# Rope attention and two MLPs on one core: k's high parts sent ahead of the low parts, and a tile of its own for the fifth unit's exponentials

## The chip, the cores and the metric

The program runs on one core of one Trainium2 chip. The metric is the device time of one execution in microseconds; the runs below are three executions of the kernel before.

## The reference, cut to what matters

```python
q_rot, k_rot = rotate(q), rotate(k)            # (4, 8, 576, 64)
scores = (q_rot @ k_rot.transpose(0, 1, 3, 2)) / sqrt(64)
scores = scores - scores.max(-1, keepdims=True)
attn = np.exp(scores)
attn = attn / (attn.sum(-1, keepdims=True) + 1e-09)
x = (attn @ v).transpose(0, 2, 1, 3).reshape(2304, 512)
h = x @ w_in                                   # 512 -> 2048
x = np.where(h >= 1, h, np.where(h <= -1, 0, (h + 1) ** 2 / 4)) @ w_out
h = np.maximum(x @ w_in2, 0)                   # 512 -> 2048
y = (s * h * h + b) @ w_out2
```

## The kernel before

All products are made from float32 numbers split into a high and a low part of the type fp32r, so that one product is three matmuls. Attention comes first, one pair of heads after the other (16 pairs, numbered 0 to 15). A pair has nine units (`UNITS`, line 333, numbered 0 to 8): 128 rows of q of one head each, and in the middle, as unit 4, the last 64 rows of both heads together. A unit goes through these steps:

- `qk` (line 338): TensorE makes a score tile `sc` of 128 by 576 in PSUM (two tiles go around), VectorE its negated row maximum `nm` (line 354), ScalarE the exponentials `p` with their row sums (line 359).
- `tmain` and `trem` (lines 363 and 383): TensorE transposes `p`. `tmain` takes four blocks of 128 columns of a unit, `trem` the remaining 128 columns of two units of a half pair; after unit 4 it also takes those of unit 4 (line 390) and is the last reader of three tiles at once.
- `av`, `inverse`, `finish` (lines 394 to 442): product with v, one over the row sums (`sume`), which GpSimd spreads out into `eb` (line 417) and TensorE transposes into `rm`; ScalarE copies that to `r` (line 433), and VectorE multiplies.

The two heads' units of the same rows share one tile `p` of 2 x 576 columns: units 0 and 1 have the first, units 2 and 3 the second, unit 4 a third, units 5 and 6 a fourth, units 7 and 8 a fifth. All come from one tag with `PB` = 3 buffers.

K of a pair is prepared during the pairs before: GpSimd multiplies and adds (`rope_pair`, line 285), and for every pair but the first `lay_k` (line 310) has ScalarE make the high part, GpSimd the low part, and SyncE's queue send them to where the score matmuls read them: the high part of each head twice to `kh` (line 323, four transfers), the low part of each head once to `kz` (line 324, two transfers). Both have two buffers, so that pair i+2's transfers wait for pair i's last score matmuls.

From unit 48 on (in pair 5) TensorE's stream also gets steps of the first MLP, called fill below (`beside`, line 472: products `h` and `y`, lines 483 and 500), and weights are converted from unit 33 on (`convert`, line 545). After attention the MLPs run alone.

The order of instructions on every engine is set when the program is built: instructions are issued in the order of the main loop (line 635), and a scheduler with its own model of time moves them, within what the tiles' buffers, the priorities and the `issue_after` marks allow. A change of a buffer thus moves instructions on all engines. Each engine then runs its stream strictly in that order.

Of the kernel before, what the change touches and what calls it, by code (L numbers as in the profile page):

```python
# [8 lines left out]
F32 = mybir.dt.float32  # L9
# [10 lines left out]
B, H, S, D = 4, 8, 576, 64  # L20
# [3 lines left out]
P = 128  # L24
# [18 lines left out]
PB = 3  # L43
# [23 lines left out]
def kernel(ctx, tc, qq, kk, vv, tab, ww1, ww2, s, b, out):  # L67
    nc = tc.nc
# [16 lines left out]
    def pool_tt(out, in0, in1, op, dim=-1):  # L85

        n = out.shape[dim]
        free = 1
        for x in out.shape[1:]:
            free *= x  # L90
        k = min(n, -(-free // PW))
        for i in range(k):
            c = [slice(None)] * len(out.shape)
            c[dim] = slice(n * i // k, n * (i + 1) // k)
            c = tuple(c)
            nc.gpsimd.tensor_tensor(out=out[c], in0=in0[c], in1=in1[c], op=op)  # L96
# [142 lines left out]
    att = pa.enter_context(tc.tile_pool(name="att", bufs=1, side="right", reuse_waits="tile"))  # L239
    att2 = pa.enter_context(tc.tile_pool(name="att2", bufs=2, side="right", reuse_waits="tile"))  # L240
# [8 lines left out]
    def bank(name):  # L249
        return ps_b.tile([P, 512], F32, tag="bank", name=name)  # L250
# [34 lines left out]
    def rope_pair(i, nm, mul, add, lo_eng, pieces=WHOLE):  # L285

        t = qk_in.pop((nm, i))
        tt = {nc.gpsimd: pool_tt, nc.vector: nc.vector.tensor_tensor}
        last = None
        for c in pieces:  # L290
            tt[mul](out=t[:, :, c], in0=t[:, :, c], in1=tab_sb[:, :, c], op=ALU.mult)
            r = t[:, 1, c]
            tt[add](out=r, in0=t[:, 0, c], in1=r, op=ALU.add)
            last = (lay_q if nm == "q" else lay_k)(i, t, c, lo_eng)
        return last

    SELF = [slice(0, D), slice(D, P)]
# [12 lines left out]
    def lay_k(i, t, c, lo_engs, heads=range(2)):  # L310
        if c.start == 0 and 0 in heads:
            stacks["k", i] = att.tile([P, 2, S], F32R, tag="kh", name="kh", bufs=2), kz_t[i % 2]
        kh, kz = stacks["k", i]
        tt = {nc.gpsimd: pool_tt, nc.vector: nc.vector.tensor_tensor}
        r = t[:, 1, c]
        if i > 0:
            hi, lo = t[:, 0, c].bitcast(F32R), r.bitcast(F32R)
            nc.scalar.copy(hi, r)
            pool_tt(out=lo, in0=r, in1=t[:, 0, c], op=ALU.subtract)
            for j in range(2):  # L320
                own = SELF[j]
                for rows in SELF:
                    nc.sync.dma_start(out=kh[rows, j, c].bitcast(F32), in_=t[own, 0, c])
                m = nc.sync.dma_start(out=kz[own, j, c].bitcast(F32), in_=t[own, 1, c])
            return m.ins
        for j in heads:
            own, other = SELF[j], SELF[1 - j]
            nc.scalar.copy(kh[own, j, c], r[own])
            m = nc.scalar.copy(kh[other, j, c], r[own])
            tt[lo_engs[j]](out=kz[own, j, c], in0=r[own], in1=kh[own, j, c], op=ALU.subtract)  # L330
        return m.ins
# [3 lines left out]
    p_t, sums_t, u_t = {}, {}, {}  # L335
    pt = {}

    def qk(i, k):
        if k == 0:
            sums_t[i] = att2.tile([P, 9], F32, tag="sums", name="sums")  # L340
        j, t = UNITS[k]
        sc = ps_s.tile([P, 2, 512], F32, tag="sc", name="sc")
        if j is None:
            places = [(0, 512), (1, S + D)]
        else:
            places = [(j, t * P + j * (QW + D))]
        straight = [[(0, 0, 288)], [(0, 288, 288)]]
        moved = [[(0, D, 288)], [(0, 352, 224), (224, 0, D)]]
        for half in range(2):
            todo = [(stacks["q", i][:, c:c + P], r[:, h], w) for h, c in places for r in stacks["k", i] for w in (moved if j is None and h == 0 else straight)[half]]  # L350
            for m, (l, r, (o, k0, n)) in enumerate(todo):
                nc.tensor.matmul(sc[:, half, o:o + n], l, r[:, k0:k0 + n], start=m == 0, stop=m == len(todo) - 1)  # L352
        nm = att.tile([P, 1], F32, tag="nm", name="nm", bufs=4)
        maxs[i * 9 + k] = nc.vector.tensor_reduce(out=nm, in_=sc[:, :, :288], axis=AX.XY, op=ALU.max, negate=True).ins  # L354
        if j != 1:
            p_t[i, t] = att.tile([P, 2 * S], F32, tag="p", name="p", bufs=PB)
        p = p_t[i, t][:, S * (j == 0):S * (j == 0) + S]
        col = 4 if j is None else 2 * t + j + t // 2
        exps[i * 9 + k] = nc.scalar.activation(p, sc[:, :, :288], AF.Exp, bias=nm, scale=1.0, accum_out=sums_t[i][:, col:col + 1]).ins  # L359
        if j is None:  # L360
            nc.scalar.copy(p_t[i, t][:, S:S + D], p[:, 512:])
# [32 lines left out]
    def av(i, g, ps, kts):  # L394

        v, n = v_in[i], GROUPS[g][1]
        r = pt["r", g]
        for kt in kts:
            for j in range(2):
                nc.tensor.matmul(ps[j * D:(j + 1) * D, :n], v[:, kt, j, :], pt[g][:, kt, j, :], start=kt == 0, stop=False)  # L400
        if 3 not in kts:
            return
        if g == 0:
            for j in range(2):
                nc.tensor.matmul(ps[j * D:(j + 1) * D, 256:320], v[:, 4, j, :], r[:, 256 + j * D:320 + j * D], start=False, stop=False)
        for j in range(2):
            nc.tensor.matmul(ps[j * D:(j + 1) * D, :256], v[:, 4, j, :], r[:, :256], start=False, stop=True)

    def inverse(i, g):

        e = att2.tile([P, 5], F32, tag="sume", name="sume")
        sm = sums_t[i]
        m = 5 - g
        nc.scalar.activation(e[:, :m], sm[:, 5 * g:5 * g + m], AF.Identity, bias=eps, scale=1.0)
        nc.vector.reciprocal(e[:, :m], e[:, :m])
        eb = att2.tile([P, 4, D], F32, tag="eb", name="eb")
        nc.gpsimd.tensor_copy(eb, e[:, 0:4].unsqueeze(2).to_broadcast([P, 4, D]))
        return e, eb

    def finish(i, g, e, eb, slices):  # L420
        ps = bank("av")
        for kts in slices:
            av(i, g, ps, kts)
            if 3 not in kts:
                yield
        rm = bank("rm")
        for t in range(2):
            nc.tensor.transpose(rm[:, t * P:(t + 1) * P], eb[:, 2 * t:2 * t + 2, :].rearrange("p j d -> p (j d)"), ident)
        if g == 0:
            nc.tensor.transpose(rm[:, 256:384], e[:, 4:5].to_broadcast([P, P]), ident)  # L430
            u_t[i] = att2.tile([P, S], F32, tag="u", name="u")
        r = att2.tile([P, 384], F32, tag="r", name="r")
        nc.scalar.copy(r[:, :384 - 128 * g], rm[:, :384 - 128 * g])
        u = u_t[i]
        c = slice(256 * g, 256 * g + 256)
        nc.vector.tensor_tensor(out=u[:, c], in0=ps[:, :256], in1=r[:, :256], op=ALU.mult)
        if g == 0:
            nc.vector.tensor_tensor(out=u[:D, 512:], in0=ps[:D, 256:320], in1=r[:D, 256:320], op=ALU.mult)
            nc.vector.tensor_tensor(out=u[D:, 512:], in0=ps[D:, 256:320], in1=r[D:, 320:384], op=ALU.mult)
            return  # L440
        bb, hp = divmod(i, NP)
        nc.sync.dma_start(out=xd[hp, :, bb * S:(bb + 1) * S], in_=u_t.pop(i))
# [79 lines left out]
    QP = [slice(0, P), slice(P, 288), slice(288, S)]  # L522
    turned_by(tk, HALVES[0])
    lay_k(0, tk, HALVES[0], [nc.gpsimd, nc.gpsimd])
    turned_by(tk, HALVES[1])
    lay_k(0, tk, HALVES[1], [nc.gpsimd, nc.gpsimd], [0])
    turned_by(tq, QP[0])
    hi, rest = lay_q(0, tq, QP[0], None, [0])
# [35 lines left out]
    def do_qk(n):  # L564
        if n < len(units):
            i, k = units[n]
            if k == 4:
                pad_v(i)
            qk(i, k)
# [28 lines left out]
    def do_t(n):  # L598
        if LT <= n < len(units) + LT:
            i, k = units[n - LT]  # L600
            tmain(i, k)
            if k in (4, 8):
                trem(i, k // 8)
                rbs[i, k // 8] = inverse(i, k // 8)
# [409 lines left out]
    def cut(n0, n1, n):  # L1014

        k = -(-(n1 - n0) // n)
        at = [n0 + (n1 - n0) // 16 * i // k * 16 for i in range(k + 1)]
        return [(a, b - a) for a, b in zip(at, at[1:])]
# [5 lines left out]
    a, b, c, d = cut(last, NT, N2A), cut(0, last, N2), cut(last, NT, N2), cut(0, NT, N2)  # L1024
# [153 lines left out]
```

## Time and profile before

| what | us |
|---|---|
| median of three runs (1125.59 to 1128.71) | 1128.46 |
| the profiled execution | 1129.47 |
| its span, first to last instruction | 1127.7 |
| TensorE busy | 1078.5 |
| VectorE busy | 786.1 |
| ScalarE busy | 631.1 |
| GpSimd busy | 430.0 |

The exponentials run from 15.5 to 434.1 us; what comes after is the MLPs. In the views, PE is TensorE, PEld its weight loads, DVE VectorE, ACT ScalarE, POOL GpSimd, SP SyncE. L359 is line 359 of the kernel. A line of the timeline has the start, the duration, the engine, and output and inputs by the program's names; a bracket gives the engine's idle time just before and what ended it. The granted clock is 1.00 at 2.4 GHz and 0.50 at 1.2 GHz.

### The profile page before, as it was taken

The page shows a single profiled execution, that of the slowest core. Times are in us where ns is not written, and L with a number is a line of the kernel's source. Part 1 is how long each engine was busy: PE and PEld are TensorE (multiplying, and loading weights), DVE is VectorE, ACT ScalarE, POOL GpSimd, SP SyncE. Part 2 cuts the span into 40 slices and gives each one's busy share as a digit, 9 for nine tenths or more (in the row PEclk, how much of TensorE's full clock was granted, in tenths as well). Part 3 has the DMA queues.
Part 4 walks back from the last instruction along what each step waited for, and adds up shares of the span by engine and source line. Part 5 has one row for each costly group of instructions (what it writes and reads, how often), then busy time and mean ns, then how long its engine had stood idle before and what let it go on. Part 6 is the DMA issues. An engine that isn't in the chain of part 4 may idle for free.

```text
span 1127.7 us, 20049 instructions
## 1 busy us (share of the span) xinstructions
PE 1078.5 (96%) x7296; PEld 986.5 (87%) x7296; DVE 786.1 (70%) x1449; ACT 631.1 (56%) x1430; POOL 430.0 (38%) x564
## 2 busy tenths in 40 slices
PE   3998988889999999999999999999999999999998
PEld 3666677778988989999999999999999999999997
DVE  6888888886676663355656667866877678767754
ACT  4777776765767665555545545465444448334421
POOL 7968886875453240252544454300211120000000
PEclk9999999999999999999999999999999999999999
DMA  7665856646667543745466573322232754221210
GB/s 221 170 183 157 243 162 190 209 150 179 199 196 217 176 157 92 265 128 180 148 222 221 193 233 113 118 74 88 80 127 90 273 183 126 82 69 54 81 62 35
DMA packets 109762, 173.24 MB, mean 154 GB/s; under 512 B 29408, under 2 KB 80608, under 8 KB 109664
## 3 DMA queue, kind: packets, MB, share of 16 engines
q1 hardware_dynamic: 109664, 171.97, 48.8%
q8 instruction: 57, 0.93, 0.3%
q14 instruction: 41, 0.34, 0.1%
HBM read 110.10 MB, written 48.56 MB: 141 GB/s over the span
## 4 chain that ended last, share of the span: by engine, by line
PE 79%; DVE 7%; DMA 4%; ACT 4%; POOL 3%; issue 2%; SPq 1%; POOLq 0%; ACTq 0%; DVEq 0%
PE hps L180 15%; PE sum L914 13%; PE yps L829 6%; PE yps L830 6%; PE yps L828 6%; PE sc L352 5%; PE y L180 4%; PE yps L764 4%; PE yps L766 4%; PE yps L765 4%; PE h L180 4%; PE av L400 3%; PE tp L374 3%; DVE nm L354 1%; POOL kin L96 1%
## 5 line engine op out<-in xcount | busy, mean ns | idle before, releaser
L180 PE MATMUL hps<-xh,w 128*128 128x288 f32 (+4 forms) x640 | 163.4, 324 | 0.0
L354 DVE TENSOR_REDUCE nm<-sc 128x1 f32<-128x576 f32 x144 | 107.9, 752 | 44.9 <-PE sc L352 44.3
L352 PE MATMUL sc<-kh,qs 128*128 128x288 f32 x336 | 104.8, 333 | 32.1 <-ACT p L359 19.7
L359 ACT ACTIVATE p<-sc,nm 128x576 f32<-128x576 f32 x144 | 106.8, 745 | 33.5 <-DVE nm L354 32.7
L922 ACT ACTIVATE four<-four,b_sb,s_sb 128x480 f32<-128x480 f32 x64 | 47.4, 782 | 127.4 <-DVE four L921 127.4
L830 PE MATMUL yps<-gh,w 128*128 128x480 f32 (+1 forms) x320 | 118.5, 370 | 0.0
L829 PE MATMUL yps<-gl,w 128*128 128x480 f32 (+1 forms) x320 | 118.5, 370 | 0.0
L828 PE MATMUL yps<-gh,w 128*128 128x480 f32 (+1 forms) x320 | 118.4, 370 | 0.0
L180 PEld LDWEIGHTS hps<-xh,w 128*128 128x128 f32 x640 | 113.2, 188 | 1.0
L96 POOL TENSOR_TENSOR wm<-wm,w 128x256 f32<-128x256 f32 x80 | 71.5, 913 | 111.9 <-ACT w L138 73.0
L352 PEld LDWEIGHTS sc<-kh,qs 128*128 128x128 f32 x336 | 65.1, 196 | 52.0 <-ACT p L359 28.6
L180 PE MATMUL hps<-xl,w 128*128 128x288 f32 (+4 forms) x320 | 103.7, 324 | 0.0
L352 PE MATMUL sc<-kz,qs 128*128 128x288 f32 x336 | 95.4, 303 | 0.0
L374 PE MATMUL tp<-ident,p 128*128 128x128 f32 x576 | 90.0, 281 | 4.9 <-ACT p L359 3.3
L764 PE MATMUL yps<-gh,w 128*128 128x288 f32 (+3 forms) x288 | 93.2, 324 | 0.7 <-ACT ys L502 0.5
L765 PE MATMUL yps<-gl,w 128*128 128x288 f32 (+3 forms) x288 | 92.8, 322 | 0.0
L766 PE MATMUL yps<-gh,w 128*128 128x288 f32 (+3 forms) x288 | 92.8, 322 | 0.0
L96 POOL TENSOR_TENSOR wm<-wm,raw 128x256 f32<-128x256 f32 x16 | 12.8, 818 | 176.9 <-ACT raw L138 176.9
L374 PEld LDWEIGHTS tp<-ident,p 128*128 128x128 f32 x576 | 72.3, 145 | 8.1 <-ACT p L359 3.7
L180 PE MATMUL y<-gh,w 128*128 128x288 f32 x320 | 75.0, 305 | 3.2 <-DVE ptr L392 2.0
L180 PE MATMUL h<-xh,w 128*128 128x288 f32 x320 | 73.3, 306 | 3.2 <-DVE gl L106 1.8
L400 PE MATMUL av<-pt,vin 128*64 128x256 f32 (+1 forms) x512 | 75.1, 417 | 0.7 <-DVE gl L106 0.7
(154 smaller groups left out, 2891.5 us busy)
## 6 DMA issues: line engine op xcount, KB each, us to landing
wraw<-in_ww SPq DMA_DIRECT2D x56, 512.0 KB, 4.4
w<-parkd SPq DMA_DIRECT2D x24, 512.0 KB, 6.3
kin<-in_k SPq DMA_DIRECT2D x15, 576.0 KB, 5.1
qin<-in_q SPq DMA_DIRECT2D x15, 576.0 KB, 4.5
kh<-kin SPq DMA_DIRECT2D x60, 144.0 KB, 2.6
parkd<-wraw SPq DMA_DIRECT2D x16, 512.0 KB, 3.1
xs<-y1d SPq DMA_DIRECT2D x32, 240.0 KB, 2.7
xd<-u SPq DMA_DIRECT2D x16, 288.0 KB, 2.6
```

The costliest lines, as they stand in the source:

```text
L180: m = nc.tensor.matmul(out_ps, l, r, start=(i == 0), stop=(i == n - 1))
L352: nc.tensor.matmul(sc[:, half, o:o + n], l, r[:, k0:k0 + n], start=m == 0, stop=m == len(todo) - 1)
L354: maxs[i * 9 + k] = nc.vector.tensor_reduce(out=nm, in_=sc[:, :, :288], axis=AX.XY, op=ALU.max, negate=True).ins
L374: m = nc.tensor.transpose(v[:, c, :], p[:, c * P:(c + 1) * P], ident)
L400: nc.tensor.matmul(ps[j * D:(j + 1) * D, :n], v[:, kt, j, :], pt[g][:, kt, j, :], start=kt == 0, stop=False)
L764: nc.tensor.matmul(acc, wh, gh, start=f == 0, stop=False)
L765: nc.tensor.matmul(acc, wh, gl, start=False, stop=False)
L766: nc.tensor.matmul(acc, wl, gh, start=False, stop=last)
L828: nc.tensor.matmul(acc, wh, gh, start=f == 0, stop=False)
L829: nc.tensor.matmul(acc, wh, gl, start=False, stop=False)
L830: nc.tensor.matmul(acc, wl, gh, start=False, stop=last)
L914: nc.tensor.matmul(acc, l, r, start=j == 0, stop=j == len(t) - 1)
```

## The change

Three things change. In `lay_k` all four transfers of the high part are issued first, and the two of the low part are marked to be issued after the last of them. Unit 4's exponentials (576 columns, and a copy of 64 of them) get a tile of their own of 640 columns with one buffer (tag `ends`), and the three buffers of `p` are left to the other units. `eb` and `r` go from two buffers to one; the 2,560 bytes per partition that this frees are those that the new tile takes.

```diff
@@ lay_k
             for j in range(2):
-                own = SELF[j]
                 for rows in SELF:
-                    nc.sync.dma_start(out=kh[rows, j, c].bitcast(F32), in_=t[own, 0, c])
-                m = nc.sync.dma_start(out=kz[own, j, c].bitcast(F32), in_=t[own, 1, c])
+                    m = nc.sync.dma_start(out=kh[rows, j, c].bitcast(F32), in_=t[SELF[j], 0, c])
+            with tc.issue_after(m.ins):
+                for j in range(2):
+                    m = nc.sync.dma_start(out=kz[SELF[j], j, c].bitcast(F32), in_=t[SELF[j], 1, c])
             return m.ins
@@ qk
         if j != 1:
-            p_t[i, t] = att.tile([P, 2 * S], F32, tag="p", name="p", bufs=PB)
+            p_t[i, t] = att.tile([P, 2 * S], F32, tag="p", name="p", bufs=PB) if t < 4 else att.tile([P, S + D], F32, tag="ends", name="p", bufs=1)
@@ inverse
-        eb = att2.tile([P, 4, D], F32, tag="eb", name="eb")
+        eb = att2.tile([P, 4, D], F32, tag="eb", name="eb", bufs=1)
@@ finish
-        r = att2.tile([P, 384], F32, tag="r", name="r")
+        r = att2.tile([P, 384], F32, tag="r", name="r", bufs=1)
```

The counts of instructions on every engine stay as they were. What follows shows how they move. Lines after 320 have other numbers in the changed kernel (359 is 360 there), the numbers behind a name tell tiles of one name apart, and "waits" names the engines (or DMA queues) whose semaphores an instruction waits for; DVE_49 is VectorE, PE_49 TensorE.

ScalarE in pair 1, around the exponentials of units 5 and 6 (tile `p_503`), before:

```order
L361 COPY p_483<-p_483 128x64 [waits Activation_49]
L414 ACTIVATE sume_543<-sums_350,eps_67 128x5
L433 COPY r_518<-rm_515 128x256 [waits PE_49]
L377 COPY pt_441<-tp_532 128x8x64 [waits PE_49]
L359 ACTIVATE p_503,sums_350<-sc_496,nm_501 128x576 [waits PE_49]
L359 ACTIVATE p_503,sums_350<-sc_522,nm_527 128x576 [waits DVE_49]
```

and in the change:

```order
L362 COPY p_483<-p_483 128x64 [waits Activation_49]
L415 ACTIVATE sume_543<-sums_350,eps_67 128x5
L360 ACTIVATE p_503,sums_350<-sc_496,nm_501 128x576 [waits DVE_49]
L434 COPY r_518<-rm_515 128x256 [waits PE_49]
L378 COPY pt_441<-tp_532 128x8x64 [waits PE_49]
L360 ACTIVATE p_503,sums_350<-sc_522,nm_527 128x576 [waits DVE_49]
```

Unit 5's exponential moved ahead of two copies that wait for TensorE, and itself waits for its maximum alone. Before, 17 of the 144 exponentials wait for TensorE, unit 5's of every pair among them; in the change it is 15, none of them in pairs 0 to 6, and in pairs 7 to 15 those of unit 2 or unit 7.

TensorE in pair 7, from unit 6's score tile (`sc_2317`) to unit 7's (`sc_2343`), before:

```order
L352 MATMUL sc_2317<-kz1_110,qs1_108 128x288
L374 MATMUL tp_2327<-ident_101,p_2247 128x128 [waits Activation_49]
L374 MATMUL tp_2327<-ident_101,p_2247 128x128 x3
L387 MATMUL tr_2333<-ident_101,p_2095 128x128 [waits DVE_49]
L387 MATMUL tr_2333<-ident_101,p_2158 128x128
L390 MATMUL tr_2333<-ident_101,p_2247 128x128 [waits Activation_49]
L352 MATMUL sc_2343<-kh_1798,qs1_108 128x288 [waits Activation_49]
```

and in the change, from the transposes of unit 4 (`p_2247`) by way of unit 8's score tile (`sc_2401`) to the first matmul of fill behind:

```order
L375 MATMUL tp_2327<-ident_101,p_2247 128x128 [waits Activation_49]
L375 MATMUL tp_2327<-ident_101,p_2247 128x128 x3
L353 MATMUL sc_2401<-kh_1798,qs1_108 128x288 [waits PE_49,Activation_49]
L353 MATMUL sc_2401<-kz1_110,qs1_108 128x288
L353 MATMUL sc_2401<-kh_1798,qs1_108 128x288
L353 MATMUL sc_2401<-kz1_110,qs1_108 128x288
L388 MATMUL tr_2333<-ident_101,p_2095 128x128 [waits DVE_49]
L388 MATMUL tr_2333<-ident_101,p_2158 128x128
L391 MATMUL tr_2333<-ident_101,p_2247 128x128
L375 MATMUL tp_2374<-ident_101,p_2288 128x128 [waits Activation_49]
L375 MATMUL tp_2374<-ident_101,p_2288 128x128 x3
L180 MATMUL h_2380<-xh_1978,w_1132 128x288 [waits DVE_49]
```

The three last transposes of the first half (`tr_2333`) stood right ahead of unit 7's score tile; now they stand behind unit 8's, and four transposes and twelve matmuls of fill follow before the next pair's first score tile. In pairs 0 to 6 TensorE's transposes stay ahead of unit 7's score tile.

SyncE's queue where pair 4's k is sent (`kin_769`), before:

```order
L324 DMA kz0_109<-kin_769 64x576 [waits DMAHW2_49,PE_49,Pool_49]
L466 DMA xs_1559<-xd_57 128x288 [waits DMAHW7_49,DMAHW3_49]
L323 DMA kh_909<-kin_769 64x576 [waits DMAHW4_49,PE_49]
L323 DMA kh_909<-kin_769 64x576 [waits DMAHW5_49]
L323 DMA kh_909<-kin_769 64x576 [waits DMAHW6_49]
L323 DMA kh_909<-kin_769 64x576
L324 DMA kz0_109<-kin_769 64x576 [waits DMAHW0_49,PE_49]
L261 DMA qin_1263<-in_q 128x1152 [waits DMAHW1_49,DVE_49]
```

and in the change:

```order
L322 DMA kh_909<-kin_769 64x576 [waits DMAHW2_49,PE_49,Activation_49]
L322 DMA kh_909<-kin_769 64x576 [waits DMAHW3_49]
L322 DMA kh_909<-kin_769 64x576 [waits DMAHW4_49]
L322 DMA kh_909<-kin_769 64x576 [waits DMAHW5_49]
L325 DMA kz0_109<-kin_769 64x576 [waits DMAHW6_49,Pool_49]
L325 DMA kz0_109<-kin_769 64x576 [waits DMAHW7_49,PE_49]
L261 DMA qin_1263<-in_q 128x1152 [waits DMAHW0_49,DVE_49]
L467 DMA xs_1559<-xd_57 128x288 [waits DMAHW1_49]
```

The first transfer of the low part went from the head of the group to behind the four of the high part, and so one transfer more lies ahead of the load of q for a later pair (`qin_1263`).

## Rows read from the trace of the kernel before

**Rows 1.** The page's first part: TensorE's busy time, share of the span and instructions.
```profile
PE 1078.5 (96%) x7296; PEld 986.5 (87%) x7296; DVE 786.1 (70%) x1449; ACT 631.1 (56%) x1430; POOL 430.0 (38%) x564
```

**Rows 2.** Stretches: busy time of each engine, instructions in brackets, granted clock, DMA.
```profile
core 0: us, PE busy (x) PEld busy (x) DVE busy (x) ACT busy (x) POOL busy (x), PEclk, DMA share, GB/s
28.00:350.00 322.00, 295.35 (x2177) 242.93 (x2176) 255.78 (x426) 224.59 (x538) 236.91 (x315) 0.98 0.64 188
350.00:1127.70 777.70, 772.82 (x5084) 734.72 (x5082) 511.95 (x997) 393.86 (x865) 172.63 (x217) 1.00 0.42 137
```

**Rows 3.** Waits of TensorE from 28 to 350 us: total, times, longest.
```profile
PE sc L352 <- ACT p L359: 17.2, 17, 2.8
PE y L180 <- POOL w L96: 0.2, 1, 0.2
```

**Rows 4.** ScalarE in order of time, pair 4: start, us, instruction.
```profile
111.26 0.75 ACT L359 ACTIVATE p<-sc,nm 128x576 f32<-128x576 f32 x1
111.99 0.74 ACT L359 ACTIVATE p<-sc,nm 128x576 f32<-128x576 f32 x1
```

**Rows 5.** TensorE at the same place; in brackets the idle time before.
```profile
110.80 0.27 PE L390 MATMUL tr<-ident,p 128*128 128x128 f32 x1
112.15 0.40 PE L352 MATMUL sc<-kh,qs 128*128 128x288 f32 x1 [1.08 <-ACT p L359]
```

**Rows 6.** VectorE at the same place.
```profile
112.99 0.76 DVE L354 TENSOR_REDUCE nm<-sc 128x1 f32<-128x576 f32 x1 [0.66 <-PE sc L352]
```

**Rows 7.** TensorE at the same place of pairs 0 and 5.
```profile
32.16 0.40 PE L352 MATMUL sc<-kh,qs 128*128 128x288 f32 x1 [1.08 <-ACT p L359]
132.63 0.40 PE L352 MATMUL sc<-kh,qs 128*128 128x288 f32 x1 [1.08 <-ACT p L359]
```

**Rows 8.** TensorE at the same place of pairs 7, 8 and 9.
```profile
188.76 0.61 PE L352 MATMUL sc<-kh,qs 128*128 128x288 f32 x1 [2.85 <-ACT p L359]
219.09 0.60 PE L352 MATMUL sc<-kh,qs 128*128 128x288 f32 x1 [2.30 <-ACT p L359]
250.23 0.61 PE L352 MATMUL sc<-kh,qs 128*128 128x288 f32 x1 [1.10 <-ACT p L359]
```

**Rows 9.** Stretches around those waits; the sixth figure is the granted clock.
```profile
185.00:188.40 3.40, 0.91 (x9) 0.67 (x6) 3.40 (x7) 3.23 (x8) 3.00 (x5) 1.00 0.16 44
188.40:191.80 3.40, 3.04 (x13) 3.03 (x14) 3.07 (x7) 2.83 (x8) 3.24 (x4) 0.50 0.16 36
219.20:222.60 3.40, 3.40 (x15) 3.37 (x16) 2.60 (x5) 2.74 (x6) 2.13 (x3) 0.51 0.95 299
249.90:253.30 3.40, 3.07 (x13) 3.06 (x14) 3.33 (x5) 3.23 (x10) 2.90 (x4) 0.51 0.47 121
277.30:280.70 3.40, 3.40 (x17) 3.38 (x16) 1.70 (x5) 2.16 (x7) 3.26 (x6) 0.52 0.26 97
```

**Rows 10.** Chain of waits: twelve matmuls of a fill step in one go.
```profile
297.12 1.59 PE h L180 x12
```

**Rows 11.** SyncE's queue in pair 2, sending pair 4's k.
```profile
72.55 0.53 SPq L324 DMA_DIRECT2D kz<-kin  x1
74.44 2.73 SPq L323 DMA_DIRECT2D kh<-kin  x4
77.28 0.55 SPq L324 DMA_DIRECT2D kz<-kin  x1
```

**Rows 12.** DMA issues, 60 to 190 us: count, KB, median us to landing.
```profile
kz<-kin SPq DMA_DIRECT2D x10, 144.0 KB, 2.7
```

**Rows 13.** TensorE, first matmul of pair 4's first score tile.
```profile
94.92 0.40 PE L352 MATMUL sc<-kh,qs 128*128 128x288 f32 x1
```

**Rows 14.** GpSimd's copy for pair 1's second group, TensorE's last transpose of the first.
```profile
57.42 0.40 POOL L417 COPY eb<-sume 128x256 f32<-128x256 f32 x1 [2.04 <-DVE sume L415]
...
60.03 0.27 PE L430 MATMUL rm<-ident,sume 128*128 128x128 f32 x1
```

**Rows 15.** Waits of GpSimd from 28 to 350 us.
```profile
POOL qin L96 <- DMA qin<-in_q: 24.5, 12, 8.5
```

## The prediction

> **What bounds the kernel now.** I read the page first: TensorE is busy for 1078.5 us of the 1127.7 us span [rows 1], so time can come only from what TensorE stands or runs slowly. The table of stretches says where. From 350 us to the end it stands for 777.7 - 772.8 = 4.9 us; from 28 to 350 us, the attention part, for 322.0 - 295.4 = 26.6 us, at a mean granted clock of 0.98 instead of 1.00 [rows 2]. The other engines have slack there: VectorE is busy for 255.8 of the 322 us, ScalarE for 224.6, GpSimd for 236.9. The list of TensorE's waits in this stretch gives the cause of most of it: 17.2 us in 17 waits end with an exponential on ScalarE, while for GpSimd it stands 0.2 us [rows 3].
>
> The timeline shows what the exponential had waited for. In pair 4, trem's last transpose starts at 110.80 [rows 5]; unit 5's exponential starts at 111.26, unit 6's right behind it at 111.99 [rows 4], though the first needs only a maximum made before. It writes a tile of `p` whose last reader was that transpose. Unit 7's score tile needs the score buffer that unit 5's exponential reads last, and TensorE stands 1.08 us before it at 112.15 [rows 5]. The same wait, 1.08 us, stands in pairs 0 to 5, six times (the first and the last in [rows 7]), and longer in pairs 7, 8 and 9: 2.85, 2.30 and 1.10 us [rows 8]. In other pairs fill lies between and hides it.
>
> **The change part by part.** *The tile of its own.* Unit 5's exponential no longer needs unit 4's tile nor the transposes behind it. In pairs 0 to 6 the order leaves no exponential waiting for TensorE. The wait of pairs 0 to 5 goes: at most 6 x 1.08 = 6.5 us. What is late next is VectorE's maximum, which had stood 0.66 us in pair 4 for that very score tile [rows 6]; the rest of the 1.08 us VectorE spent on work that must be done anyway. I take 6 x 0.66 = 3.9 us, since the steps behind hang on VectorE, and keep 0 (the next step simply waits elsewhere) and 6.5 as ends.
>
> In pairs 7 to 15 the same step is moved, not removed: 15 exponentials (units 2 and 7) there wait for a group of transposes that the order now puts later. What counts is how much TensorE has to do between those transposes and the score tile that needs the exponential. Before, it had nothing in pairs 7 and 8 and nine matmuls (1.59 / 12 x 9 = 1.2 us [rows 10]) in pair 9, so that transposes to score tile took 2.85, 2.30 and 1.10 + 1.2 = 2.3 us [rows 8], 2.5 in the mean. In the changed order 12 of the 15 have a step of twelve matmuls or its worth behind them, 1.59 us, mostly two; three (pair 11, unit 7; pair 13, unit 7; pair 15, unit 2) have about 1.2 us. If all took 2.5 us, the three would cost 3 x 1.3 = 3.9 us and the two with little over 1.6 us (pair 7, unit 7; pair 8, unit 2) about 0.6 each: 5.0 us. As several pairs before hid the wait with as little, I take half, 2.5 us. So of 2.85 + 2.30 + 1.10 = 6.25 us, 3.75 are won; ends 1.25 and 6.25.
>
> *The clock.* Each of the three long waits has a stretch at 1.2 GHz on it: the granted clock is 1.00 from 185.0 to 188.4 us, in which TensorE worked for 0.91 us, and 0.50 from 188.4 to 191.8; so it is again at 219.2 and 249.9, and a fourth time at 277.3, where no exponential was waited for [rows 9]. In the first three TensorE is busy 3.04, 3.40 and 3.07 us; at 2.4 GHz that work takes half, so they cost 1.52 + 1.70 + 1.54 = 4.8 us. I take two of the three, 3.2 us, as the moved order can bring one of its own; ends 0 and 4.8, with the fourth (1.7) 6.5. The Trainium skill ("TensorE: Matmul & The Clock Gate", Part 1: The HAM clock gate) says that the low clock is the default state, which activity lifts and idleness brings back. By that rule all three would go with their waits, 4.8 us instead of 3.2, and the total would be 1117.0; the trace agrees as far as the place goes, since every low stretch begins beside an idle TensorE.
>
> *High parts first.* Nobody waits for these transfers. Pair 4's are issued from 72.55 to 77.28 + 0.55 [rows 11] and land 2.7 us later [rows 12], at 80.5; its first score matmul starts at 94.92 [rows 13]. The first transfer of `kh` must wait for pair 2's last score matmuls anyway, and `kz` ahead of it ran in that pause. Now both `kz` come behind: one transfer, 0.55 us, is added ahead of the next load of q. GpSimd stands 24.5 us in 12 waits for such loads [rows 15], so 12 x 0.55 = 6.6 us more at worst for GpSimd; TensorE waits for GpSimd for 0.2 us in all [rows 3]. I cost it at nothing; what hides it is the lead of more than 14 us that k has, and GpSimd's 322 - 237 = 85 us of idle time.
>
> *One buffer for `eb` and `r`.* `eb` of a pair's second group must now wait for the transposes of the first group's. In pair 1 the copy starts at 57.42 and those transposes end at 60.03 + 0.27 = 60.30 [rows 14]: it would stand 2.9 us. Behind it in GpSimd's queue is the low part of a k that is sent only at 72.55 [rows 11]: 11 us of cover. Nothing, by the same idle time; if that were gone, 16 x 2.9 = 46 us of GpSimd against its 85. `r` is written once in half a pair and read by VectorE within that half: nothing.
>
> **The sum.** 3.9 + 3.75 + 3.2 = 10.9 us. Against the profiled execution, 1129.5 - 10.9 = **1118.6 us**; that execution lies 1.0 us above the median of the runs, which is within what the runs differ by.
>
> **The rivals.**
> - *All of it.* TensorE keeps the whole of the waits, and no low clock replaces the three: 6.5 + 6.25 + 4.8 = 17.5 us, 1112.0; with the fourth stretch and a part of the unrelated waits (26.6 - 17.2 = 9.4 us in the stretch, which a new order shuffles) down to 1109. For it: all other engines have slack in the sums. Against: the steps behind unit 7 are VectorE's.
> - *The stall only moves.* In pairs 0 to 5 VectorE's maximum is met by other work of VectorE, and in pairs 7 to 9 the new waits cost the upper 5.0 us with one or two low stretches: 6.25 - 5.0 + about 0, some 1 us, **1128**. For it: one exponential in ten still waits for TensorE, 15 against 17 before. Against: the 15 are those with fill behind them.
> - *Slower, by the late transposes.* Trem now stands behind two score tiles in most of pairs 7 to 15, and the fill that should hide the wait has inputs from ScalarE's same queue, in which the exponential stands. If it stands too, the cover is gone. With seven of the 15 uncovered at the mean of rows 8, 2.08 us, that is 14.6 us, and 7 x 1.6 = 11.2 us of low clock; less 3.9 + 6.25 + 4.8 = 14.95 that go, 10.9 us slower, **1140.4**. It decides from about four uncovered waits on: 4 x (2.08 + 1.6) = 14.7. Against: before, no wait with twelve matmuls behind it showed.
> - *The first part does something.* It can't help: the data lie there 14 us early.
>
> **How the numbers follow.** A measurement here can tell about 0.3%, 3.4 us, from no change. My forecast has 0.46, with a range of its own from 1114 to 1124; all of it 0.18; the moved stall 0.20; slower 0.16. Faster by over 0.3% (under 1125.1): 0.46 + 0.18 + 0.02 of the moved stall = 0.66; the rest of it, 0.18, is within; slower 0.16. The range leaves out the slower case and a little below: 1109 to 1130.
>
> **What would show it.** Right, if the trace after has: unit 5's exponential apart from unit 6's in pairs 0 to 6, with no wait of TensorE of 1.08 us before unit 7's score tile; the sum of TensorE's waits on exponentials from 28 to 350 us at half of 17.2 us or less; one or two low-clock stretches instead of four; and the span from 350 us on unchanged. Wrong, if waits of 1 us and more stand before the first or the third score tile of pairs 8 to 15, if VectorE's idle time in the first 150 us does not fall, or if GpSimd's wait for `rm` at `eb` reaches TensorE.

## The result, and the profile after

The changed kernel takes 1114.26 us in the median of four runs (1113.05 to 1114.57), the kernel before 1127.03 us beside it (1125.18 to 1128.71): a ratio of **0.9883, 95% interval 0.9865 to 0.9901**. The forecast was 1118.6 us. The profiled executions differ by 1129.47 - 1114.57 = 14.9 us, the medians by 12.8, and the readings below are made against the 14.9 of the profiles.

The page's first part and two lines of its table of groups, changed kernel (to [rows 1]; in a group's line the last figures are idle time before it and what ended most of it):

```profile
PE 1074.0 (97%) x7296; PEld 982.0 (88%) x7296; DVE 778.2 (70%) x1449; ACT 628.5 (56%) x1430; POOL 431.1 (39%) x564
...
L360 ACT ACTIVATE p<-sc,nm 128x576 f32<-128x576 f32 x144 | 106.7, 743 | 32.1 <-DVE nm L355 29.5
...
L355 DVE TENSOR_REDUCE nm<-sc 128x1 f32<-128x576 f32 x144 | 106.7, 749 | 22.6 <-PE sc L353 21.9
```

VectorE's maxima stand 21.9 us for score tiles; the same line of the kernel before had this:

```profile
L354 DVE TENSOR_REDUCE nm<-sc 128x1 f32<-128x576 f32 x144 | 107.9, 752 | 44.9 <-PE sc L352 44.3
```

The stretches, changed kernel, as in [rows 2], and then split where pair 6's first exponential starts:

```profile
28.00:350.00 322.00, 306.55 (x2300) 252.16 (x2300) 260.69 (x449) 233.03 (x563) 243.83 (x322) 1.00 0.66 198
350.00:1112.80 762.80, 757.22 (x4964) 721.14 (x4960) 499.80 (x976) 382.81 (x840) 167.44 (x210) 1.00 0.41 136
28.00:134.34 106.34, 102.60 (x740) 74.43 (x739) 96.38 (x157) 82.22 (x193) 96.71 (x125) 1.00 0.69 198
134.34:1112.80 978.46, 961.16 (x6522) 898.87 (x6520) 664.10 (x1267) 533.61 (x1212) 314.55 (x408) 1.00 0.46 149
```

The same split of the kernel before:

```profile
28.00:141.74 113.74, 103.97 (x753) 74.52 (x751) 98.32 (x160) 83.24 (x194) 96.01 (x127) 1.00 0.67 189
141.74:1127.70 985.96, 964.19 (x6508) 903.14 (x6506) 669.42 (x1264) 535.21 (x1210) 313.53 (x406) 0.99 0.46 148
```

This split is the sum in measured form. A stretch's length less TensorE's busy time is its idle time. Up to pair 6 TensorE's idle time falls from 9.8 to 3.7 us and its busy time by 1.4, as 13 of its instructions now come later. Behind that point idle time falls from 21.8 to 17.3 us and busy time by 3.0, although the 13 instructions are added. Together: 6.0 + 4.5 = 10.5 us of idle time and 4.4 us of busy time. The instructions are the same 7296, so the 4.4 us are instructions that ran faster: the granted clock is 1.00 in every stretch, and none of the four stretches of [rows 9] is left. (The record of the clock begins at 28.0 us in the kernel before and at 31.0 in the changed one. Up to there a score matmul with `kz` takes 0.44 us, behind it 0.29 to 0.30, so the changed kernel's first 3 us in the table are slow ones that the figure 1.00 does not show.)

The waits of TensorE from 28 to 350 us, changed kernel, its two longest sums (to [rows 3]), and of GpSimd's those of [rows 14, 15]:

```profile
PE sc L353 <- ACT p L360: 7.0, 10, 1.4
PE tp L375 <- DVE pt L382: 2.6, 3, 1.7
...
POOL qin L96 <- DMA qin<-in_q: 19.5, 8, 8.1
...
POOL eb L418 <- PE rm L429: 4.4, 3, 2.4
```

TensorE waits for exponentials 7.0 us instead of 17.2. The three longest of these waits that are left:

```profile
110.51 0.40 PE L353 MATMUL sc<-kh,qs 128*128 128x288 f32 x1 [1.20 <-ACT p L360]
...
124.39 0.40 PE L353 MATMUL sc<-kh,qs 128*128 128x288 f32 x1 [0.82 <-ACT p L360]
...
180.15 0.40 PE L353 MATMUL sc<-kh,qs 128*128 128x288 f32 x1 [1.42 <-ACT p L360]
```

The first stands at the end of pair 4, for unit 7's exponential, where the kernel before has no such wait; the last stands in pair 7, for unit 6's. The place itself, in pair 2 of the changed kernel (exponentials of units 5 and 6; TensorE's last transpose of `trem` and unit 7's score tile; VectorE's maxima of units 6 and 7), to be held against [rows 4 to 6]:

```profile
67.27 0.74 ACT L360 ACTIVATE p<-sc,nm 128x576 f32<-128x576 f32 x1 [0.72 <-DVE nm L355]
68.73 0.77 ACT L360 ACTIVATE p<-sc,nm 128x576 f32<-128x576 f32 x1
...
68.22 0.27 PE L391 MATMUL tr<-ident,p 128*128 128x128 f32 x1
68.25 0.38 PE L353 MATMUL sc<-kh,qs 128*128 128x288 f32 x1
...
67.85 0.71 DVE L355 TENSOR_REDUCE nm<-sc 128x1 f32<-128x576 f32 x1
69.28 0.74 DVE L355 TENSOR_REDUCE nm<-sc 128x1 f32<-128x576 f32 x1
```

Unit 5's exponential starts 0.95 us ahead of the last transpose and 1.46 us ahead of unit 6's (0.73 before), so that unit 7's score tile follows the transpose without a pause, where 1.08 us stood.

### The profile page after: what moved, and what is told of

It reads as the page before. It is cut to its first block, busy times and chain, and to the rows that moved or that the text cites. A ratio compares the mean times of both kernels' runs of the same rounds, so it can differ in the third digit from the quotient of the medians.

```text
span 1112.8 us, 20049 instructions
## 1 busy us (share of the span) xinstructions
PE 1074.0 (97%) x7296; PEld 982.0 (88%) x7296; DVE 778.2 (70%) x1449; ACT 628.5 (56%) x1430; POOL 431.1 (39%) x564
## 4 chain that ended last, share of the span: by engine, by line
PE 82%; DVE 7%; DMA 3%; ACT 3%; POOL 3%; issue 2%; SPq 0%; POOLq 0%; ACTq 0%; DVEq 0%
PE hps L180 15%; PE sum L915 14%; PE yps L831 6%; PE yps L830 6%; PE yps L829 6%; PE y L180 5%; PE sc L353 5%; PE yps L765 4%; PE av L401 4%; PE yps L767 4%; PE yps L766 4%; PE h L180 4%; PE tp L375 3%; DVE nm L355 2%; ACT p L360 1%
## 5 line engine op out<-in xcount | busy, mean ns | idle before, releaser
L355 DVE TENSOR_REDUCE nm<-sc 128x1 f32<-128x576 f32 x144 | 106.7, 749 | 22.6 <-PE sc L353 21.9
L96 POOL TENSOR_TENSOR wm<-wm,raw 128x256 f32<-128x256 f32 x16 | 12.8, 819 | 176.5 <-ACT raw L138 176.5
L375 PEld LDWEIGHTS tp<-ident,p 128*128 128x128 f32 x576 | 70.8, 143 | 10.2 <-ACT p L360 3.7
L106 DVE TENSOR_TENSOR gl<-hps,gh 128x288 fp32r<-128x288 f32 (+4 forms) x88 | 46.5, 528 | 40.5 <-ACT gh L102 40.4
```

What stands on the lines that cost most here:

```text
L375: m = nc.tensor.transpose(v[:, c, :], p[:, c * P:(c + 1) * P], ident)
```

## The experiments

The theory: the tile of its own makes the gain, in two places, by the waits of pairs 0 to 5 and by those of pairs 7 to 9 with their stretches at 1.2 GHz; the other two parts are worth nothing. The rivals: one of the other parts does something; or the tile does nothing in one of the places, and the gain there is that of another order of instructions, since the scheduler moves instructions on all engines after any edit. So the first five kernels (e1 to e5) are parts of the change; the rest test the order (by a second rate of fill), the size of the early gain, and more cover. The kernels with the tile in some pairs only (e3, e4, e9, e12) have the other two parts as well.

All results in one table. "Begins" is the start of pair 6's first exponential, "behind" the rest of the span; "idle" (TensorE's idle time) and "1.2 GHz" are for that rest, the latter by the record of the granted clock, without the end of the program. "Unit 5" is the sum of TensorE's waits (0.15 us and longer) from pair 7 on that end with an exponential of unit 5, as read from each trace. All these are of one profiled execution; the ratio is that of the runs to the kernel before.

| kernel | tile in pairs | begins | behind | idle | unit 5 | 1.2 GHz | ratio (95%) |
|---|---|---|---|---|---|---|---|
| before | none | 141.7 | 986.0 | 21.8 | 6.8 | 13.7 | 1 |
| e2_kz_only | none | 139.8 | 988.5 | 24.1 | 7.2 | 13.7 | 1.0033 (1.0019 to 1.0046) |
| e5_single_only | none | 141.5 | 989.6 | 23.1 | 7.1 | 20.5 | 1.0043 (1.0027 to 1.0059) |
| e6_before_fill | none | 141.2 | 986.0 | 25.6 | 3.5 | 3.4 | 1.0033 (1.0021 to 1.0045) |
| e4_late_only | 7 to 15 | 143.0 | 982.1 | 18.6 | 0.5 | 13.7 | 1.0002 (0.9989 to 1.0015) |
| e9_three | 0 to 2 | 135.7 | 991.2 | 23.6 | 6.2 | 20.5 | 1.0006 (0.9991 to 1.0022) |
| e3_early_only | 0 to 6 | 134.9 | 983.3 | 19.7 | 5.1 | 10.2 | 0.9925 (0.9902 to 0.9948) |
| e12_early_fill | 0 to 6 | 133.6 | 985.5 | 23.7 | 3.5 | 3.4 | 0.9966 (0.9948 to 0.9984) |
| the changed kernel | all | 134.3 | 978.5 | 17.3 | 0.6 | 0 | 0.9883 (0.9865 to 0.9901) |
| e1_no_kz | all | 134.8 | 986.1 | 20.7 | 0 | 13.7 | 0.9946 (0.9925 to 0.9967) |
| e7_after_fill | all | 134.3 | 982.0 | 19.7 | 0 | 6.8 | 0.9909 (0.9893 to 0.9925) |
| e8_nokz_fill | all | 133.2 | 983.2 | 19.2 | 0 | 10.2 | 0.9912 (0.9897 to 0.9926) |
| e10_fill80 | all | 135.5 | 984.2 | 21.7 | 0 | 10.2 | 0.9954 (0.9940 to 0.9968) |
| e11_fill70 | all | 133.7 | 993.8 | 26.1 | 0 | 20.5 | 1.0036 (1.0020 to 1.0052) |

### The parts, one by one

**k's transfers in the old order, all else as changed (e1), and the new order alone (e2).** In e1 the two `kz` transfers go back between those of `kh`, as the minus lines of the change's first hunk have them; e2 is the kernel before with the plus lines of that hunk alone.

> The changed kernel with the transfers of k put back into their old order; the tile of its own and the single buffers stay. Theory (the gain is the exponential's wait and the clock on it; nobody waits for k's transfers): as fast as the changed kernel, 1113 to 1116 us, no 1.08 us wait in pairs 0 to 5, none or one low-clock stretch. Rival (sending the high parts first is part of the gain): 1118 us or more.

> The kernel before with k's high parts sent first and nothing else changed. Theory: no change, 1125.5 to 1129 us, with the waits of 1.08 us in pairs 0 to 5 and three or four low-clock stretches still there. Rival (the transfers give part of the gain): 1123 us or less.

Measured: 1120.96 us and 1131.45 us. Neither fits the theory, and e1's time is what the rival had said: without the part the changed kernel loses 6.7 us. But alone the part loses 0.33%. Two signs for one edit do not speak for an effect on the chip; they speak for the order. That is put to the test by e7 and e8 below.

**The tile in the early pairs alone (e3), in the late ones alone (e4).** In pairs without it unit 4 takes one of the three tiles `p`, as before. This is e3's condition; e4 has `i < 7` in the place of `i > 6`.

```diff
...
-if t < 4 else att.tile([P, S + D], F32, tag="ends", name="p", bufs=1)
+if t < 4 or i > 6 else att.tile([P, S + D], F32, tag="ends", name="p", bufs=1)
```

> The changed kernel with unit 4's own tile in pairs 0 to 6 only; from pair 7 on unit 4 takes one of the three buffers of p again. Theory: the early part of the gain alone, 4 to 8 us, so 1119 to 1123 us; pair 6 begins at about 134 us as in the changed kernel; unit 5's exponential waits again in pairs 7 to 9 and the low-clock stretches there are back. Rival (the gain is not in the waits but in the new order of conversions and fill behind): the gain is not split, 1115 us or less, or 1126 and more.

> The changed kernel with unit 4's own tile from pair 7 on only. Theory: the late part of the gain alone, 5 to 9 us, so 1118 to 1122 us; six waits of 1.08 us in pairs 0 to 5 as in the kernel before, and none or one low-clock stretch behind. Rival: as for the run before, 1115 us or less, or 1126 and more.

Measured: 1119.87 us and 1126.78 us. The split of e3's profile, and of e4's:

```profile
28.00:134.90 106.90, 101.08 (x734) 72.37 (x733) 97.11 (x157) 81.54 (x191) 95.81 (x125) 1.00 0.68 197
134.90:1118.20 983.30, 963.64 (x6522) 903.30 (x6521) 664.97 (x1267) 534.54 (x1212) 316.02 (x408) 0.99 0.47 148
```

```profile
28.00:142.96 114.96, 103.85 (x744) 74.78 (x743) 101.06 (x162) 84.36 (x195) 97.21 (x129) 0.99 0.65 187
142.96:1125.10 982.14, 963.55 (x6518) 903.50 (x6516) 661.26 (x1263) 533.55 (x1210) 311.33 (x404) 0.99 0.46 148
```

E3 is as expected: pair 6 begins as early as in the changed kernel, and what lies behind is nearer to the kernel before. Unit 5's exponential is waited for again in pairs 7 and 8 (2.35 and 2.09 us), though not in pair 9. E4 missed its time. Its split shows 982.1 us behind pair 6 against 986.0, and unit 5's late waits are down to 0.5 us; but it runs 13.7 us at 1.2 GHz there, as the kernel before does, where at most one stretch had been expected. It gives 1.2 us back in pairs 0 to 5, where it should be as before, and the medians show no gain (1.0002). The change in the early part is worth most; the late one needs a better test (e12).

**One buffer for `eb` and `r` alone (e5).** The kernel before with `bufs=1` at both, as in the change.

> The kernel before with eb and r at one buffer each and nothing else changed. Theory (GpSimd's wait for the transposes is hidden by its idle time): no change, 1125.5 to 1130 us, GpSimd waits for rm at eb for some 3 to 10 us in all, and TensorE for GpSimd for under 1 us. Rival (that wait reaches TensorE): 1132 us or more.

Measured: 1132.94 us. Waits of GpSimd from 28 to 350 us in e5, the one of this kind that the kernel before has there, and those of TensorE in e5:

```profile
POOL eb L417 <- PE rm L430: 11.9, 1, 11.9
...
POOL eb L417 <- PE rm L428: 6.8, 1, 6.8
```

```profile
POOL eb L417 <- PE rm L430: 5.5, 1, 5.5
```

```profile
PE sc L352 <- ACT p L359: 18.9, 15, 3.5
...
PE y L180 <- POOL w L96: 0.2, 1, 0.2
```

The waits for `rm` are there, 18.7 us in two where the kernel before stands 5.5 once, and one is 11.9 us long where the prediction had 2.9. The time is one that the rival had said (1132 or more). But TensorE still waits for GpSimd for 0.2 us in all, so the wait does not reach it directly; what grew is TensorE's waits for exponentials, 18.9 us instead of 17.2, and its time at 1.2 GHz, 23.9 us in all instead of 13.7. The miss is of the size of an order drawn anew, and this part alone was not run at a second order: that the single buffers cost some of the 0.43% is not excluded.

### Is it the order? A second rate of fill

`run_fill` sets how many steps of fill are let in for each unit, 0.62 in pairs 5 to 8 and 0.92 behind. A slightly other rate leaves the work as it is and makes the scheduler draw the order behind the start of pair 6 anew: in the traces TensorE's order first differs at 150.7 us between the kernel before and e6, and at 144.7 us between the changed kernel and e7, and that of the other engines later still. So these kernels test the late part; the early part has the same order at both rates. Three kernels with the new rate stand to each other as before, after and e1 do.

```diff
-            run_fill(0.62 if n < 76 else 0.92)
+            run_fill(0.6 if n < 76 else 0.9)
```

> The kernel before with the fill per unit at 0.6 and 0.9 instead of 0.62 and 0.92, which hardly changes the work beside attention but makes the scheduler find another order from pair 5 on. It is the base of the two runs that follow. Theory (what follows pair 6 depends on the order that is found, by some 4 us either way): 1123 to 1132 us, pair 6 begins at 140 to 143 us. Rival (the order does not matter by itself): 1126 to 1129 us.

> The changed kernel with the same fill. Theory: pair 6 begins at 134 to 136 us as in the changed kernel, 6 to 8 us earlier than in the run before; the rest is 976 to 988 us by the order found, so 1111 to 1124 us in all. Rival (the tile and the high parts first together bring what the changed kernel showed, whatever the order): 1113 to 1116 us, and no low-clock stretch.

> The same fill, with the tile and the single buffers, and k's transfers in the old order. Theory (the transfers' order matters only through the order of everything else that the scheduler finds): pair 6 begins at 134 to 136 us; the total lies within 4 us of the run before, on either side. Rival (high parts first is worth some 6 us beside the tile, on the chip itself): 5 to 8 us slower than the run before.

Measured: 1130.96 us for the kernel before with this rate, 1117.14 for the changed one and 1116.98 for the changed one with k's old order. So the whole change is worth 13.8 us here, as much as at the first rate (12.8). Sending the high parts first is worth nothing here (0.9909 against 0.9912), as predicted, so that the 6.7 us of e1 are best read as those of an order. How much an order can do shows among kernels that differ in the rate and the other two parts alone: those without the tile (before, e2, e5, e6) lie up to 0.43% apart, those with the tile in all pairs (the changed kernel, e1, e7, e8) up to 0.63%. In both groups the fastest is the one by which the change was measured. Still the slowest with the tile (0.9946) is faster than the fastest without.

E12 then takes the late tile away at this rate (the diff is e3's on top of e7's):

> The changed kernel with the second fill rate (0.60 and 0.90), with unit 4's own tile in pairs 0 to 6 alone. It stands to the changed kernel at that rate as the run with the tile in the early pairs stood to the changed kernel: a second pair that differs in the late tile only. Theory (the late tile is worth some 4 to 5 us by itself, as in the first pair, 983.3 against 978.5 us behind the start of pair 6): pair 6 begins at 133 to 135 us, 985 to 988 us lie behind it, against 982.0 with the late tile; ratio to the kernel before 0.994 to 0.998. Rival (the late tile is worth nothing; the first pair differed by the order that was drawn): 978 to 983 us behind pair 6, ratio 0.987 to 0.992.

```profile
28.00:133.60 105.60, 101.67 (x739) 73.28 (x739) 96.52 (x157) 82.22 (x192) 96.80 (x125) 1.00 0.69 199
133.60:1119.10 985.50, 961.78 (x6522) 900.49 (x6520) 668.12 (x1267) 534.24 (x1212) 313.37 (x408) 1.00 0.46 148
```

Measured: 1123.63 us, ratio 0.9966, and 985.5 us behind pair 6 against e7's 982.0: as the theory had it. The late tile is now taken away or added in three pairs of kernels: 986.0 to 982.1 (before and e4, which also differ in the other two parts), 983.3 to 978.5 (e3 and after), 985.5 to 982.0 (e12 and e7). It is worth 3.9, 4.8 and 3.5 us behind pair 6. Each of these is the difference of two single executions, and those of the kernel before alone lie between 1122.7 and 1131.5 us; by the ratios of the runs it is worth 0.42% (e3 and after) and 0.57% (e12 and e7), and nothing shows between before and e4. Over all kernels of the two rates the time behind pair 6 is 978.5 to 986.1 us with the late tile (five kernels) and 983.3 to 991.2 without (seven): the ranges overlap, so the size is known only roughly. What no order blurs is the wait itself: unit 5's late waits are 0 to 0.6 us in all seven kernels with the late tile and 3.5 to 7.2 in all seven without.

### How large is the early gain, and what holds the rest?

**The tile in pairs 0 to 2 alone (e9)**, the condition of e3 with `i > 2`.

> Changed kernel, but unit 4 takes its own tile in pairs 0 to 2 alone; from pair 3 on it takes one of the three as before. Theory (each early wait of 1.08 us comes through whole, one by one): three of six waits go, so pair 6 begins 3 to 4 us before the 139.8 to 143.0 us of the kernels without the tile, at 136.5 to 138.5 us, and TensorE keeps three waits of 1.08 us in pairs 3 to 5. The late part then has no tile: 983 to 990 us behind it; time 1121 to 1129. Rival (the early gain is one thing that the tile sets off in pair 0, or one that needs all of the pairs): pair 6 begins at 134 to 135 or at 140 and later.

Measured: 1127.38 us, pair 6 at 135.7, between what theory and rival had said; the 991.2 us behind it are a little above the forecast. The rows say more than the sum. Pairs 0, 1 and 2 last 22.1, 18.8 and 18.3 us, as in the changed kernel (22.1, 18.7, 18.4); pair 3, the first without the tile, 21.5, as before (21.9; 18.4 in the changed kernel), with the wait back at its place. TensorE's waits in e9's pair 3:

```profile
87.14 0.40 PE L353 MATMUL sc<-kh,qs 128*128 128x288 f32 x1 [1.08 <-ACT p L360]
91.39 0.40 PE L353 MATMUL sc<-kh,qs 128*128 128x288 f32 x1 [0.46 <-ACT p L360]
94.32 0.40 PE L353 MATMUL sc<-kh,qs 128*128 128x288 f32 x1 [1.00 <-ACT p L360]
```

So in pair 3 the effect comes and goes with the tile, in every kernel here (17.7 to 18.4 us with it, 21.0 to 21.9 without). But it is not 1.08 us in each pair: from the kernel before to the changed one, pairs 0 to 5 become shorter by 0.9, -0.1, 2.4, 3.4, -0.2 and 1.2 us. In pair 4 the new wait of 1.20 us at 110.51 takes the place of the old one; why pairs 2 and 3 gain more than their wait was not followed up. That e9's pair 5 lasts only 19.1 us without the tile stays open; it has less fill in it (6 matmuls against 12 in the kernel before).

**More fill in pairs 5 to 8 (e10: 0.8 and 0.92; e11: 0.7 and 1.0)**, to cover the waits that are left, and to beat both kernels.

> Changed kernel with more fill steps put into pairs 5 to 8 (0.80 of the rate instead of 0.62). Theory (what is left between the changed kernel and its bound is TensorE's waiting for exponentials in pairs 5 to 9, which fill covers): idle time of TensorE from 28 to 350 us falls from 15.5 us by 1 to 3, time 1111 to 1114. Rival (each small edit draws another order, whose late part differs by some 4 us either way, and cover isn't what is lacking): 1114 to 1120, idle time unchanged or longer.

> Changed kernel with somewhat more fill in pairs 5 to 8 (0.70 instead of 0.62) and behind (1.0 instead of 0.92). Theory (cover): between the changed kernel and the one with 0.80, 1111 to 1114. Rival (another order drawn): anywhere from 1112 to 1120, with no trend over the rates 0.60/0.90, 0.62/0.92, 0.70/1.0 and 0.80/0.92.

Measured: 1121.74 and 1130.01 us, both slower than the changed kernel (1114.26) and above what even the rivals had said; no version here beats it. TensorE's waits for exponentials did fall, from 7.0 to 4.3 and 4.6 us, but others took their place, in e10 one of 4.75 us for VectorE's `pt` in pair 12: TensorE's idle time from 28 to 350 us rose from 15.5 to 18.9 and 19.3 us. E11 shows what else there is to lose, at the passage from attention to the MLPs. Its stretch from 420 to 470 us:

```profile
420.00:470.00 50.00, 44.69 (x310) 38.94 (x309) 13.89 (x31) 21.67 (x58) 9.45 (x13) 0.90 0.44 146
```

Two of the waits of TensorE in it, from e11's timeline:

```profile
452.71 0.40 PE L180 MATMUL hps<-xh,w 128*128 128x288 f32 x1 [1.41 <-ACT xh L102]
455.19 0.61 PE L180 MATMUL hps<-xl,w 128*128 128x288 f32 x1 [2.08 <-POOL xl L96]
```

The same stretch of the changed kernel:

```profile
420.00:470.00 50.00, 49.46 (x380) 47.46 (x377) 18.20 (x39) 24.41 (x64) 15.41 (x19) 1.00 0.59 196
```

TensorE waits there for the parts of x that ScalarE and GpSimd split, and runs 10.2 us at 1.2 GHz; 70 of its instructions fewer are done in the same 50 us. The passage itself lies earlier in the changed kernel, whose last exponential ends at 416.1 us and not at 435.0; in the 50 us that lie to it as these do to e11's, from 401.1 to 451.1, its TensorE stands 0.15 us at a clock of 1.00.

## Why the prediction was right, and where it was off

The direction, the waits that would go and their place were right, and the time lies in the range, 0.3 us above its lower end. The sum was short by 4 us, 10.9 against 14.9 in the profiled executions (12.8 by the medians). The 4 us are 2.1 of early waits, 0.75 of late ones and 1.2 of the clock.

- *Early waits: 3.9 taken, 6.0 measured.* This is the term that was mis-sized most. The step that failed is that each wait would give only the 0.66 us that VectorE had stood in pair 4 [rows 6], the rest being held by VectorE's own work. VectorE had far more slack: it stood 113.74 - 98.32 = 15.4 us in this part and stands 106.34 - 96.38 = 10.0 us now; for score tiles it waits 21.9 us instead of 44.3 in the whole program. One pair's wait was a poor sample: by pairs the gain runs from nothing to 3 us. All nine kernels with the tile in the first pairs begin pair 6 at 133.2 to 135.7 us, all five without at 139.8 to 143.0. The five have four different orders up to there (before and e6 share one), the nine at least three; none of these orders bridges the gap.
- *Late waits: 3.75 taken, 4.5 us of idle time measured behind pair 6.* The mechanism was right: unit 5's waits from pair 7 on fall from 6.8 to 0.6 us. The 2.5 us set aside for the exponentials of units 2 and 7 did not come: from pair 7 on TensorE waits for none of them, and its longest wait for any exponential is 1.42 us, for unit 6's in pair 7, against 2.85 before. Other waits took a part of what was won. (For pair 9 the prediction counts 2.3 us from transposes to score tile; another 1.02 us, in which TensorE stood for `ptr` at 247.64 us, lie between.)
- *The clock: 3.2 taken, 4.4 us less busy time measured (3.0 of it behind pair 6).* Two stretches of three were to go; all four went, and at a lower price than was taken. That they went with the waits is not shown, and their part of the gain looks like luck of the order that the change got: the seven kernels with the late tile run 0 to 20.5 us at 1.2 GHz behind pair 6, the seven without 3.4 to 20.5; e4 lost unit 5's late waits and kept 13.7 us. With the second rate the same change shortens that part by 986.0 - 982.0 = 4.0 us instead of 7.5. As for the price, the forecast took a stretch of about 3.4 us as 1.5 to 1.7 us lost; by that all four would be worth 6.5 us, and busy time fell by 4.4. E6 lost three of four stretches and was no shorter behind pair 6 (986.0), as its idle time grew by 25.6 - 21.8 = 3.8 us. Over 194 runs of before and the experiments, compared within each kernel, a run is 0.26 us (0.05 either way at 95%) longer for each us at 1.2 GHz in its mean clock, about half of what the forecast used. That a part of the slow work lies where TensorE would have waited anyway would explain it, and was not tried by itself.
- *The rule on the clock.* From the Trainium skill ("TensorE: Matmul & The Clock Gate", Part 1: The HAM clock gate), by which the low clock is the default state that activity lifts, the prediction drew that every stretch would go with its wait. All three did in the changed kernel. But a long wait does not always bring a stretch: e6 waits 2.74 us for unit 5's exponential of pair 6 at 158.71, and its granted clock stays 1.00, with less of TensorE's work around the wait (0.66 us) than the 0.91 that stood ahead of the first slow stretch of [rows 9]:

```profile
155.40:158.80 3.40, 0.66 (x7) 0.42 (x4) 2.06 (x4) 3.39 (x10) 3.40 (x7) 1.00 0.02 8
158.80:162.20 3.40, 3.40 (x27) 3.23 (x29) 2.62 (x5) 3.40 (x9) 1.47 (x2) 1.00 0.57 143
```

- *High parts first, nothing:* borne out by e7 and e8; not visible from e1 and e2, whose orders differ by more. TensorE's list of waits names no transfer of k in either kernel, and GpSimd's waits for loads of q, which were to grow by up to 6.6 us, went from 24.5 to 19.5.
- *One buffer for `eb` and `r`, nothing:* neither shown nor refuted. In the changed kernel GpSimd stands 4.4 us for `rm` from 28 to 350 us, 24.3 in all, and TensorE never waits for GpSimd; but e5, the only run with this part alone, is 0.43% slower.
- *The rivals.* "All of it" (1112.0) came nearer than the forecast: 2.6 us off against 4.0. The early waits went almost whole (6.0 of 6.5) and all stretches with them, though up to half of the late saving was an order's luck. The moved stall and the late transposes did not come: from pair 8 on TensorE's longest wait for an exponential is 0.59 us.
- *What would show it.* Unit 5's exponential apart from unit 6's and waits on exponentials at 7.0 of 17.2 us: as forecast. The span from 350 us on, forecast as unchanged, fell from 777.7 to 762.8 us, since 123 instructions more are done by then; TensorE's idle time in it is much as it was (4.9 and 5.6 us). The stretches: none instead of one or two.

What stays open: how much of the ratio 0.9883 another order would take away. With the second rate the changed kernel stands at 1117.14 us, and e10 and e11 lie above that again, while the gain against a kernel before of the same rate is 12.8 and 13.8 us. Open too are what the single buffers cost and how large the late gain is.

## What to carry to other kernels

Where one instruction's buffer waits for the last reader of a shared set of tiles, a small tile of its own frees it. How much of the wait is won can't be read from one instance of the next engine's wait; here that engine's slack over the whole stretch was the better guide. Where a scheduler orders the program, an edit that seems to do nothing on the chip moved the time by anything from 0 to 6.7 us. Three things told an effect from such a draw: a second setting that leaves the work as it is, a split of the span at a fixed piece of work, and the one wait that the edit is about, counted in every trace.

## What was not expected of the hardware

Time at 1.2 GHz cost less than the 1.5 to 1.7 us for each 3.4 us that half the clock would give: 0.26 us for each us at that clock over 194 runs, though this is a comparison of runs and not a trial. One program also differs from run to run in it: e12's twelve runs have mean clocks from 0.994 to 1.000, and take 1118.69 and 1120.44 us at 1.000, 1124.49 to 1127.70 us at 0.994 and 0.995, a spread of 9.0 us. The changed kernel's four runs, at 0.998 to 1.000, lie within 1.5 us. So one profile with or without such a stretch is one draw.
